# Chunk-selected attention and a squared-ReLU feed-forward on one core: every engine's order and the order of the loads fitted anew, and another price for a constant row copy

## Chip, cores and metric

The kernel runs on one core of one Trainium2 chip. The metric is the device time of one execution in microseconds (us), lower is better. The engines of a core are TensorE (PE in the profile), VectorE (DVE), ScalarE (ACT), GpSimd (POOL) and SyncE (SP). Each takes its instructions strictly in the order in which they were written for it; they wait for one another by semaphores.

## What is computed

The reference, cut to what matters (4 batches, 8 heads, 768 positions, 64 values a head; 3072 tokens, 512 wide, 2048 hidden):

```python
k_min, k_max = min and max of k over each chunk of 32 keys
ub = sum_d max(q*k_min, q*k_max)             # a bound on a chunk's scores
ub = where(chunk not after the query's, ub, -1e9)
sel = the 6 chunks with the largest ub, for each query
scores = where(sel and key <= query, (q @ k.T) / 8, -1e9)
attn_out = softmax(scores) @ v               # batch, head, position
x = attn_out as (3072, 512)
out = relu(x @ w_in)**2 @ w_out
```

## The kernel before

**Tiling.** A batch has six tiles of 128 positions. The first tile of each batch needs no selection; `first_transposes` and `first_attention` (L553 to L606) do the four of them at the start, and one feed-forward pass takes them together. The other five tiles go through 16 pairs of heads, numbered p = 0 to 15, four to a batch. `stage_a(p)` (L622 to L739) prepares a pair: keys and queries turned so that the 64 values lie on partitions (on PE in batches 0 and 1, by a transposing DMA of SP in batches 2 and 3), chunk extremes (`kr`, L697), the bounds on PE (`ub`, L660), the sixth largest of them (`m`, L668), the selection (`selb`, L727), turned as well (`sT`), and copies into the operands `kqc` and `qsc` (L281 on ACT, L283 on DVE). `stage_b(p, x)` (L766 to L821) then does, for each of the two heads, five banks of scores (`ps`, L782), the exponential on ACT (`e`, L804), the causal mask on POOL (L762) or DVE (L759), and the product with v (`av`, L793), at last the division (L612, L614) into `x`.

`ffn` (L823) runs once for the first tiles and once for each batch: `turn` (x to xT; by PE, or by SP's transposing DMAs for batches 1 to 3), `up` (`ph`, L866; ReLU `ht` on ACT, L873, or DVE, L875; square `h` on DVE, L884), `down` (`py`, L897; a copy `ob`, L281 or L283; a store by SP, L910). The feed-forward of a batch lies between and behind the attention of the next.

**The selection as a product.** The operand `kqc` has 64 rows of keys and 24 constant rows that add a large negative number for every chunk that isn't selected. These 24 x 768 constant rows are made once (L339) and copied seven times for the eight operands, the "row copies": L344 on POOL, L281 on ACT, L283 on DVE.

**What sets the order.** The kernel is written as some 1800 operations with no order of their own. `plan.op` records each with the engines it may run on and a price for each, a due time, what it needs and the buffers it uses. `Plan.order` then goes through them like a list scheduler in a model of the chip: it finds the operation that could start first, and on that engine takes, among those that could start within `wait` of it, the one with the smallest due time:

```python
first = min(found, key=lambda f: (f[0], f[1].number))
st, op, engine, cost = min(
    (f for f in found if f[2] == first[2] and f[0] <= first[0] + self.wait),
    key=lambda f: (round(f[1].due, 6), f[0], f[1].number))
```

What comes out is the order of each engine's queue, the engine for each operation that has a choice, and the buffer slots (three of `ps`, six of `e`, six of `nt`, two each of `av` and `ff`). Loads from memory are operations of POOL, whose order among themselves is the list `plan.loads`; the planner takes the next of that list when its due time beats what else POOL could do, and lets at most eight be under way. Before the 26th microsecond of its model, `Plan.order` also puts idle matmuls in front of a PE operation that must wait (`op.fill`, L539, "fillers"), to keep PE busy. They are as many as its model of the wait says; where the wait is shorter than that, they stand in the way. The due times come from a table of numbers, `P`, near the top of the kernel, and from places in a timetable of 20 units for each pair.

Loads that the prediction speaks of: the weights `w_in` in four chunks (L461), keys, queries and values of batch 0 by pairs of heads (`kn`, `qn`, `vn`, L454), first tiles of each batch (`k`, `q`, `v`, L369), whole tiles of batch 1 (L447), and `nt`, the tiles of keys and queries that SP turns by DMA for batches 2 and 3 (L434). Four first tiles (`raw`, L399) are fetched by SP itself and cast by DVE or ACT.

Of the kernel before, what the change touches and what calls it, by code (L numbers as in the profile page):

```python
# [13 lines left out]
ACT = mybir.ActivationFunctionType  # L14
# [194 lines left out]
def kernel(  # L209
# [27 lines left out]
    QC = 128 * NS  # L237
    VW = 80
    NSET = 4
    P = dict(lead=[0, 207.45, 109.14, 153.29, -29.2, 112.12, 38.49, 53.35, 112.23, 30.95,  # L240
             26.44, 98.99, 127.21, 67.89, -1.38, 124.88], f_due=[452.52,
             -1393.33, -782.42, -326.54], sp='K0 Q0 K1 Q1', rows=[-2963.23,
             -1559.78, 780.78, -565.55, 1811.92, 457.36, -1818.66, -283.78],
# [3 lines left out]
             'q3 v2 v3 k3', shift={}, p0=-2735.84, wait=0.01, xt=(1, 2, 3),  # L247
             sel=2, loads='Q3 K3 V0 V1 Q2 K2 i0 V2 k0 V3 q0 i1 k1 v2 q1 i2 '
             'v0 i3 k2 q2 o1 o0 v1 o2 k3 o3 v3 q3')

    nc.scalar.preload_act_table_set("natural_log_exp_and_others")

# [13 lines left out]
    plan = Plan({"tp": 1, "ps": 3, "av": 2, "ff": 2, "e": 6, "h2": NFI + 6, "ht": 3,  # L266
                 "ob": 3, "kq": 6, "nt": 6,
                 "vn": B - 1, "x": 2, "xT": 2,
                 "st": 2, "kr": 2, "qp": 2, "qm": 2, "ubm": 2, "m8": 2, "rc": 2}, lambda *a: keep_warm(*a), P["wait"])
    POOLS = {"tp": pst, "ps": pss, "av": psav, "ff": psf, "e": epool, "h2": hpool,  # L270
# [65 lines left out]
    def kq_rows(engine, i):  # L336
        rows = kqs[D:KC, i // 2, i % 2]
        if i == 0:
            nc.scalar.activation(  # L339
                rows.rearrange("c (a j) -> c a j", j=CH),  # L340
                ident[0:NC, 0:NC].unsqueeze(2).to_broadcast([NC, NC, CH]),
                ACT.Copy, scale=NEG)
        elif engine == "POOL":
            nc.gpsimd.affine_select(  # L344
                out=rows, in_=kqs[D:KC, 0, 0], compare_op=ALU.is_ge, fill=0.0,
                base=0, channel_multiplier=0, pattern=[[1, S]])
        else:
            copy(engine, rows, kqs[D:KC, 0, 0])

    made = {}  # L350
# [7 lines left out]
    order = []  # L358
# [93 lines left out]
    def load_pair(nm, b, hp, due):  # L452
        for h in (2 * hp, 2 * hp + 1):
            load((nm, b, hp), lambda _, h=h: nc.gpsimd.dma_start(  # L454
                out=nat[nm, b].tile[:, :, h, 0:D],
                in_=SRC[nm][b, h, 128:].rearrange("(j p) d -> p j d", p=128)),
                due, 640, [nat[nm, b]])
# [21 lines left out]

    for i, what in enumerate(P["sp"].split()):  # L480
        if what[0].isupper():
            load_by_sp(what[0].lower(), int(what[1]), -1020 + i)
        else:
            load_pair_by_sp(what[0], -1020 + i)
    made["ident"] = plan.op({"POOL": 0.75}, -997, lambda _: make_identity(nc, ident))
    made["ahead"] = plan.op({"POOL": 0.55}, -994, make_ahead)
    made["rows", 0] = plan.op({"ACT": 0.88}, P["rows"][0], lambda e: kq_rows(e, 0),
                              [made["ident"]])
    for i in range(1, 2 * NSET):
        made["rows", i] = plan.op({"POOL": 0.80, "DVE": 0.40, "ACT": 0.75}, P["rows"][i],  # L490
                                  lambda e, i=i: kq_rows(e, i), [made["rows", 0]])
    made["tri"] = plan.op({"DVE": 0.15}, -900, lambda _: nc.vector.tensor_single_scalar(
        tri, ahead, 0.0, op=ALU.is_ge), [made["ahead"]])
# [1 line left out]
    made["ubmask"] = plan.op({"DVE": 0.8}, -997, make_ubmask)  # L495
    for what in P["loads"].split():
        i = int(what[1])
# [6 lines left out]
        else:  # L504
            load_pair(what[0], 0, i, -980)
    if P["after"]:
        plan.loads[0].needs.append(made["rows", P["after"]])
# [21 lines left out]
    def keep_warm(dst, n):  # L529

        size = 1
        for dim in dst.shape[1:]:
            size *= dim
        dst = dst if len(dst.shape) == 2 else dst.rearrange(
            {3: "p a b -> p (a b)", 4: "p a b c -> p (a b c)"}[len(dst.shape)])
        if dst.dtype == F32:
            size = min(size, 512) // 128 * 128 or size
            for _ in range(n * 512 // size):
                nc.tensor.matmul(  # L539
                    dst[:, 0:size].rearrange("p (a b) -> p a b", b=min(size, 128)),  # L540
                    lhsT=warm, rhs=warm[:, 0:min(size, 128)].unsqueeze(1).to_broadcast(
                        [128, size // min(size, 128), min(size, 128)]),
                    start=True, stop=True)
        else:
            for _ in range(4 * n):
                transpose(dst[:, 0:128], warm)
# [412 lines left out]
    computed = [op for op in plan.ops if op.turns or not op.packets]  # L959
    for i, change in P["shift"].items():  # L960
        computed[i].due += change
    with tc.manual_schedule():
        plan.write()

# [29 lines left out]
```

## Time and profile before

| | |
|---|---|
| median of 3 runs | 265.79 us (264.72, 265.79, 266.02) |
| profiled execution | a span of 263.6 us from the first to the last instruction; the page gives no other time of it |
| mean granted clock of TensorE | 0.994 |
| busy: PE, DVE, ACT, POOL | 251.4, 183.0, 197.8, 106.4 us |
| instructions | 6555 |

The timed runs lie 1.1 to 2.4 us above the span of the profiled execution. Busy time counts an instruction from its start to its end; matmuls overlap their ends, so a PE that is shown as busy all the time is not at its peak. A row of a group has the line of the source, the engine, the operation, the tiles out<-in with their shapes and the count, then busy us and mean ns of one, then the idle time of the engine ahead of it and what ended most of that. Windows have, for each stretch, busy us and instructions of each engine, the granted clock of PE, and the mean use of the DMA engines.

### The profile page before, as it was taken

Reading aid. Unit: us, or ns where it says so; the run is one execution under the profiler, and the core shown is the slowest. Engines: PE = TensorE matmul, PEld = TensorE weight load, DVE = VectorE, ACT = ScalarE, POOL = GpSimd, SP = SyncE. Lnnn points to the kernel's source line nnn. Section 1 sums busy time; section 2 is a strip of 40 time slices with the busy share of each in tenths; the row PEclk is TensorE's granted clock in tenths of the full one; section 3 lists DMA queues with packets and bytes.
Section 4 is the critical chain, followed back from the end, with each engine's and each line's share of the span. In section 5 each row is a group of like instructions: output and inputs, shape, how many; then the busy total and the mean of one; then the engine's idle time right before and its main releaser. Section 6 shows DMA issues by size and latency. Waiting matters only on the chain.

```text
span 263.6 us, 6555 instructions
## 1 busy us (share of the span) xinstructions
PE 251.4 (95%) x2382; PEld 164.1 (62%) x2405; DVE 183.0 (69%) x663; ACT 197.8 (75%) x395; POOL 106.4 (40%) x185
## 2 busy tenths in 40 slices
PE   6899999999999999999999999998999999999995
PEld 1577566666687666665686645666865564765443
DVE  7569999778999999998999943644757142455000
ACT  6658897859899999999989845987866692677111
POOL 7998987799555599833311201110200010000000
PEclk9799999999999999999999999999999999999999
DMA  8999999999999999995440001154000113400122
GB/s 153 156 175 180 181 198 190 94 126 174 170 151 166 149 157 143 123 145 148 87 93 15 2 20 75 44 82 101 2 0 15 42 44 99 120 2 0 40 82 80
DMA packets 106336, 26.51 MB, mean 101 GB/s; under 512 B 99008, under 2 KB 103360, under 8 KB 106304
## 3 DMA queue, kind: packets, MB, share of 16 engines
q0 software_dynamic: 75088, 13.11, 67.9%
q1 hardware_dynamic: 31216, 12.98, 24.0%
q8 instruction: 19, 0.31, 0.5%
q14 instruction: 13, 0.11, 0.2%
HBM read 27.26 MB, written 6.29 MB: 127 GB/s over the span
## 4 chain that ended last, share of the span: by engine, by line
PE 62%; DVE 24%; ACT 8%; issue 3%; DMA 2%; SPq 0%; ACTq 0%; DVEq 0%
PE py L897 25%; PE ph L866 20%; PE ps L782 8%; PE av L793 4%; DVE h L884 4%; DVE kr L697 4%; DVE m L668 3%; DVE qsc L283 3%; ACT e L804 2%; DMA xT<-x 2%; ACT ht L873 2%; DVE x L614 2%; ACT qsc L281 2%; DVE kqc L283 1%; DVE ubm L722 1%
## 5 line engine op out<-in xcount | busy, mean ns | idle before, releaser
L866 PE MATMUL ph<-xT,w_in_sb 128*128 128x256 bf16 (+2 forms) x592 | 95.7, 304 | 1.6 <-DMA xT<-x 1.2
L804 ACT ACTIVATE e<-ps 128x512 bf16<-128x512 f32 x160 | 86.4, 608 | 7.5 <-PE ps L782 4.4
L897 PE MATMUL py<-w_out_sb,h 128*128 128x512 bf16 (+2 forms) x377 | 87.9, 370 | 1.2
L762 POOL TENSOR_SCALAR_AFFINE_SELECT e<-e 128x128 bf16<-128x128 bf16 (+1 forms) x88 | 31.0, 365 | 101.0 <-ACT e L804 89.1
L866 PEld LDWEIGHTS <-w_in_sb 128*128 128x128 bf16 x592 | 55.6, 97 | 24.9 <-DMA xT<-x 1.6
L873 ACT ACTIVATE ht<-ph 128x384 bf16<-128x384 f32 (+2 forms) x130 | 58.9, 457 | 16.2 <-PE ph L866 12.5
L884 DVE TENSOR_TENSOR h<-ht 128x256 bf16<-128x256 bf16 (+2 forms) x148 | 47.8, 333 | 16.4 <-ACT ht L873 12.9
L897 PEld LDWEIGHTS <-h 128*128 128x128 bf16 x400 | 36.2, 97 | 33.8
L782 PE MATMUL ps<-qsc,kqc 88*128 88x128 bf16 (+1 forms) x320 | 51.7, 272 | 0.3 <-DVE ubm L722 0.2
L782 PEld LDWEIGHTS <-kqc 88*128 88x128 bf16 x320 | 27.6, 97 | 14.8 <-issue 0.8
L281 ACT COPY ob<-py 128x512 f32<-128x512 f32 (+2 forms) x22 | 12.5, 570 | 29.2 <-PE py L897 29.1
L793 PEld LDWEIGHTS <-e 128*128 128x128 bf16 x640 | 29.6, 97 | 6.4 <-issue 0.3
L793 PE MATMUL av<-vn,e 128*128 128x65 bf16 x480 | 29.6, 193 | 0.0
L759 DVE TENSOR_TENSOR e<-e,tri 128x128 bf16<-128x128 bf16 (+1 forms) x40 | 9.7, 242 | 14.9 <-ACT e L804 14.2
L614 DVE TENSOR_TENSOR x<-av,rc 128x320 bf16<-128x320 f32 (+1 forms) x40 | 18.7, 472 | 0.5
L668 DVE MAX8 m<-ubm 128x8 f32<-128x24 f32 x160 | 15.5, 167 | 0.0
L697 DVE TENSOR_REDUCE kr<-kT 128x24 bf16<-128x768 bf16 x16 | 14.8, 951 | 0.2
L697 DVE TENSOR_REDUCE kr<-kt 128x24 bf16<-128x768 bf16 x16 | 14.8, 935 | 0.0
L793 PE MATMUL av<-v,e 128*128 128x65 bf16 x160 | 13.9, 193 | 0.1
L875 DVE TENSOR_SCALAR ht<-ph 128x256 bf16<-128x256 f32 (+2 forms) x18 | 8.2, 454 | 8.2 <-PE ph L866 8.2
L612 DVE RECIPROCAL rc<-av 128x5 f32<-128x5 f32 (+1 forms) x40 | 7.2, 184 | 9.4 <-PE av L793 8.5
L281 ACT COPY qsc<-sT 24x256 bf16<-24x256 bf16 (+1 forms) x29 | 12.4, 427 | 1.6 <-DMA sT<-selb 0.9
(92 smaller groups left out, 258.7 us busy)
## 6 DMA issues: line engine op xcount, KB each, us to landing
out_dram<-ob SPq DMA_DIRECT2D x23, 256.0 KB, 2.2
w_in_sb<-in_moe_w_in_dram POOLq DMA_DIRECT2D x4, 512.0 KB, 7.2
w_out_sb<-in_moe_w_out_dram POOLq DMA_DIRECT2D x4, 512.0 KB, 8.8
vn<-in_v_dram POOLq DMA_DIRECT2D x15, 128.0 KB, 6.9
nt<-in_k_dram POOLq DMA_DIRECT2D x10, 128.0 KB, 6.6
nt<-in_q_dram POOLq DMA_DIRECT2D x10, 128.0 KB, 5.3
kn<-in_k_dram POOLq DMA_DIRECT2D x8, 80.0 KB, 7.0
qn<-in_q_dram POOLq DMA_DIRECT2D x8, 80.0 KB, 5.7
```

What stands on the lines that cost most here:

```text
L281: nc.scalar.copy(dst, src)
L614: return plan.op({"DVE": 0.06 + 0.00108 * D * n}, due, lambda _: nc.vector.tensor_mul(x(), av[:, :, 0:D], rc[:, 0:n].unsqueeze(2).to_broad ...
L668: nc.vector.max(out=m8[:, i, hh], in_=ubm[:, i, hh])
L697: nc.vector.tensor_reduce(kr[:, mm].rearrange("d (t c) -> d t c", c=128 // CH) if b >= BY_DMA else kr[:, mm], part(kT).rearrange("d t (c j ...
L762: nc.gpsimd.affine_select(out=e, in_=e, compare_op=ALU.is_ge, fill=0.0, base=0, channel_multiplier=-1, pattern=[[0, n], [1, 128]])
L782: nc.tensor.matmul(ps[:, 128 * c:128 * (c + nt)], lhsT=kqs[:, s, hh, 128 * j:128 * (j + 1)], rhs=qss[:, s, hh, 128 * (t0 - 1):128 * (t0 - ...
L793: nc.tensor.matmul(av[:, t - 1], lhsT=e[:, 128 * c:128 * (c + 1)], rhs=value_tile(b, h, j), start=(i == 0 and c == 0), stop=(i == len(BANK ...
L804: nc.scalar.activation(e.tile, ps.tile, ACT.Exp, scale=scale), [sc], [ps, e])
L866: nc.tensor.matmul(ph.tile, lhsT=w_in_sb[:, ki, 128 * f:128 * (f + 1)], rhs=xT[:, c0 // 128:c1 // 128, ki], start=(ki == 0), stop=(ki == N ...
L873: nc.scalar.activation(ht.tile, ph.tile, ACT.Relu)
L884: {"DVE": 0.067 + w / 1920}, at[0] + P["h2"], lambda _: nc.vector.tensor_mul(h2[f][:, c0:c1], ht.tile, ht.tile), [op], [ht, h2[f]])))
L897: nc.tensor.matmul(py.tile, lhsT=h2[f][:, 128 * t:128 * (t + 1)], rhs=w_out_sb[:, f, c0:c1], start=(f == 0), stop=(f == NFI - 1))
```

## The change

Two things change in the table and one in a price; no computation changes, and no operation is added or taken away.

- `P["moves"]`: some 150 triples (first, last, change). Each adds a number to the due times of a run of operations that stand one after another in the program, from one operation to a few dozen or a hundred.
- `P["order"]`: another order for the 85 loads in `plan.loads`.
- the price of a row copy on DVE, 0.40 before, is 0.80; `wait` goes from 0.01 to 0.01025.

```diff
+    P.update(moves=[(404, 421, -16.62), (1023, 1024, 27.61), (1310, 1388, 35.65),
+             (1004, 1029, 6), (1072, 1086, -0.87), (1539, 1540, 6.97), (1535, 1536,
...
+             17.64)], order=[0, 2, 3, 1, 5, 4, 6, 10, 9, 8, 7, 12, 11, 13, 14, 15,
+             19, 16, 18, 20, 17, 22, 21, 23, 25, 30, 26, 24, 27, 29, 34, 31, 28, 33,
...
+             wait=0.01025)
...
     for i in range(1, 2 * NSET):
-        made["rows", i] = plan.op({"POOL": 0.80, "DVE": 0.40, "ACT": 0.75}, P["rows"][i],
+        made["rows", i] = plan.op({"POOL": 0.80, "DVE": 0.80, "ACT": 0.75}, P["rows"][i],
                                   lambda e, i=i: kq_rows(e, i), [made["rows", 0]])
...
     computed = [op for op in plan.ops if op.turns or not op.packets]
     for i, change in P["shift"].items():
         computed[i].due += change
+    for i0, i1, change in P["moves"]:
+        for op in computed[i0:i1]:
+            op.due += change
+    if P["order"]:
+        plan.loads = [plan.loads[i] for i in P["order"]]
```

Set beside each other, the two programs differ in this: of 1809 operations 96 run on another engine; of PE's 642 operations 184 keep their place in its queue and 245 more stand within three places of it; PE has 2399 matmuls instead of 2405, since 22 fillers at L539 are left of 28. In the first microseconds the first tile of batch 1 now comes ahead of that of batch 0. In the last batch, the attention of pair 14 and 15 comes earlier against the feed-forward of the batch before it.

More of the change, by code (lines that the diff above doesn't have):

```diff
@@ L239 @@
     NSET = 4
-    P = dict(lead=[0, 207.45, 109.14, 153.29, -29.2, 112.12, 38.49, 53.35, 112.23, 30.95,
+    P = dict(moves=[], order=[], lead=[0, 207.45, 109.14, 153.29, -29.2, 112.12, 38.49, 53.35, 112.23, 30.95,
              26.44, 98.99, 127.21, 67.89, -1.38, 124.88], f_due=[452.52,
```

42 rows, old and new, of the table sel are left out of this document.

## Prediction

> **What bounds the kernel now.** I read the page's head first, then the windows by stage, then what PE waited for, and last the timeline of the start, since PE is the engine that is nearly always busy.
>
> ```profile
> span 263.6 us, 6555 instructions
> PE 251.4 (95%) x2382; PEld 164.1 (62%) x2405; DVE 183.0 (69%) x663; ACT 197.8 (75%) x395; POOL 106.4 (40%) x185
> ...
> 0.00:24.00 24.00, 19.36 (x193) 13.05 (x194) 16.84 (x59) 15.98 (x26) 21.45 (x34) 0.93 1.69 163
> 24.00:70.00 46.00, 44.94 (x483) 28.90 (x487) 41.15 (x147) 37.77 (x73) 40.54 (x62) 1.00 1.68 165
> 70.00:130.00 60.00, 58.58 (x629) 40.12 (x634) 58.34 (x204) 57.84 (x115) 35.73 (x65) 1.00 1.70 143
> 130.00:260.20 130.20, 128.34 (x1085) 81.97 (x1093) 66.67 (x256) 85.92 (x182) 8.71 (x26) 1.00 0.18 48
> 260.20:263.60 3.40, 0.20 (x4) 0.02 (x1) 0.00 (x0) 0.27 (x1) 0.00 (x0) 1.00 0.22 77
> ```
>
> The columns of a window are its length, then busy us of PE, PEld, DVE, ACT and POOL with instructions, then the granted clock and the DMA traffic. PE is idle for 263.6 - 251.4 = 12.2 us: 4.64 before the 24th microsecond, 3.2 in the tail of the last store, which no order shortens, and 1.06, 1.42 and 1.86 in the three stages between, 4.3 in all. So an order can win some 9 us at the very most, and in practice a part of that. From 70 to 130 three engines are full together (58.58, 58.34 and 57.84 of 60).
>
> ```profile
> PE T L286 <- DVE k L283: 1.8, 1, 1.8
> PE ph L866 <- DMA xT<-x: 1.2, 1, 1.2
> PE xt L286 <- ACT kqc L281: 0.5, 1, 0.5
> PE ub L660 <- DVE kbd L704: 0.4, 1, 0.4
> ```
>
> These are the longest waits of PE for other engines and transfers (in all, times, longest). The first lies in the start; the one of 1.2 us is a transposing DMA that came late; then come crumbs. No stall repeats, so a refit of orders has no big prize, and the fullness of the middle gives it something to lose.
>
> **The change part by part.** PE does the same work but for six fillers, and these stand before the first feed-forward's first products for tiles 2 and 3. Behind that point the PE work is equal, so the end moves by what the start moves plus waits that come or go.
>
> *The start.* PE's rows from the 15th microsecond and ACT's up to the 24th:
>
> ```profile
> 15.74 1.70 PE L539 MATMUL ph<-warm 128*128 128x256 bf16 x14
> 17.28 1.04 PE L866 MATMUL ph<-xT,w_in_sb 128*128 128x256 bf16 x8
> 19.80 1.60 ACT L281 COPY kqc<-kT 64x768 bf16<-64x768 bf16 x2
> 20.52 0.44 PE L286 MATMUL qT<-ident,qn 128*128 128x128 bf16 x5
> 21.43 1.39 ACT L281 COPY qsc<-qT 64x640 bf16<-64x640 bf16 x2
> 21.68 1.69 PE L539 MATMUL ph<-warm 128*128 128x256 bf16 x14
> 22.84 0.59 ACT L281 COPY xT<-xt 128x512 bf16<-128x512 bf16 x1
> 23.47 1.03 PE L866 MATMUL ph<-xT,w_in_sb 128*128 128x256 bf16 x8
> ```
>
> Here are the four loads that matter: the first chunk of `w_in`, the last first tile `v`, and the queries `qn`, with one landing row for each of the three in that order.
>
> ```profile
> 9.39 0.79 POOL L461 DMA_DIRECT2D w_in_sb<-in_moe_w_in_dram  x1
> DMA to landing us min/median/max: 6.7/6.7/6.7
> 12.71 0.96 POOL L369 DMA_DIRECT2D v<-in_v_dram  x1
> DMA to landing us min/median/max: 6.8/6.8/6.8
> 13.59 1.79 POOL L454 DMA_DIRECT2D qn<-in_q_dram  x2
> DMA to landing us min/median/max: 5.8/5.9/6.1
> 1.83 0.44 POOL L422 MEMSET vn<- 128x40 bf16 x2
> ```
>
> Before, `w_in` lands at 9.39 + 6.7 = 16.1, yet the first product starts at 17.28, because 14 fillers (15.74 to 17.44, ends overlapped) stand in the way. After, POOL does one more memset of 0.22 (0.44 / 2) ahead of its loads, which was DVE's, so they start 0.2 to 0.4 later: the chunk lands near 9.7 + 6.7 = 16.4, and only 6 fillers stand ahead of the product. It starts at 16.4 to 16.6, 0.8 earlier. I don't believe that this gain is kept. The second `qn` is issued half-way through its row, at 14.49 before and about 14.7 after, and lands at 14.7 + 5.9 = 20.6 instead of 20.4. It feeds `qT` of pair 0, and behind that ACT has, in its strict order and in both kernels, the two `qsc` copies (1.39) and then an `xT` copy (0.59), for which the second products of `up` wait: 0.12 from the landing to the first transpose (20.52 against 20.4), 0.44 for them, and I allow 0.15 for the hand-overs: 20.6 + 0.71 + 1.39 + 0.59 = 23.3, against 23.43 (22.84 + 0.59) before. The 14 fillers ahead of them (1.69) end at about the same time. So the start gains 0.15: the whole 0.8 at one end; at the other a loss of 0.3, if the loads are late by their 0.4 and nothing takes it up.
>
> Row copies and casts:
>
> ```profile
> 2.97 2.29 ACT L281 COPY kqc<-kqc 24x768 bf16<-24x768 bf16 x3
> 5.96 0.91 DVE L283 CAST k<-raw 128x512 bf16<-128x512 f32 x1
> ```
>
> The doubled price sends one row copy from DVE to ACT (0.76 a copy, 2.29 / 3), two left on DVE. The cast of a key tile goes to ACT as well. Both engines have gaps there (16.84 and 15.98 busy of 24), and PE is held by loads; I cost this at nothing, covered by the load of `w_in`. If that cover is gone, a copy that stands ahead of an exponential costs its 0.76; this I leave to the slower case.
>
> *The loads behind the start.* The page's DMA row, and the last keys of batch 1, with their landing row and first use:
>
> ```profile
> DMA  8999999999999999995440001154000113400122
> 51.78 1.79 POOL L447 DMA_DIRECT2D kn<-in_k_dram  x2
> DMA to landing us min/median/max: 3.4/4.4/5.3
> 58.91 0.44 PE L286 MATMUL kT<-ident,kn 128*128 128x128 bf16 x5
> ```
>
> The second of them, issued at 52.67, lands 3.4 to 5.3 later, 58.0 at the latest, 0.9 before its use. After, it is issued about 1.1 earlier, and the first `nt` loads some 5 earlier. This removes no wait of 24 to 130 that I can name, only a part of the 2.5 us of crumbs; I take -0.3, between nothing and -1.0. By the Trainium skill, page "DMA: Bandwidth & Descriptors", section "Issuing engines are not separate DMA queues", transfers from all issuers interleave on the same 16 engines, so a load moved ahead only pushes others back. The DMA row's nines up to slice 18 agree, and by that rule alone this term would be 0.
>
> *Pairs 0 to 7, 24 to 70.* Most PE operations move a few places. One move forward matters: the fifth score bank of pair 1's second head now stands about 4 us earlier, near 43, where the exponentials
>
> ```profile
> L804 ACT ACTIVATE e<-ps 128x512 bf16<-128x512 f32 x160 | 86.4, 608 | 7.5 <-PE ps L782 4.4
> ```
>
> must free three `ps` slots at 0.608 each. If ACT is one late there, PE waits for up to one, 0.6; I take +0.2.
>
> *70 to 130.* The engines of 36 operations are swapped: 18 from ACT to DVE, 17 back, one POOL to DVE.
>
> ```profile
> L875 DVE TENSOR_SCALAR ht<-ph 128x256 bf16<-128x256 f32 (+2 forms) x18 | 8.2, 454 | 8.2 <-PE ph L866 8.2
> L283 DVE COPY qsc<-sT 24x384 bf16<-24x384 bf16 (+1 forms) x35 | 10.0, 285 | 1.3 <-PE sT L286 0.5
> ```
>
> ReLUs, seven to DVE and three back: 4 x 0.454 = +1.8 on DVE. Selection copies, three to DVE and seven back: -4 x 0.285 = -1.1. The other sixteen are net two more on DVE at up to 0.5 each, 0 to +1.0. DVE gets +0.7 to +1.7, I take +1.2; it is idle for 60 - 58.34 = 1.66. It fits, barely: 0. Bounds: -1.4, the whole idle time of PE there; and, if DVE can use none of its idle time, +1.2 to +1.7, say +1.4.
>
> *130 to the end.*
>
> ```profile
> DMA to landing us min/median/max: 2.4/2.5/5.2
> 175.44 5.17 DMA xT<-x
> ```
>
> These are the transposing DMAs of batch 2's `xT` and the late one. PE's work that covers that place is, by its queue, much the same in both kernels, so the wait of 1.2 depends on whether the transfer is late again: usually it takes 2.5. Its neighbours, not its place, decide it; I leave it in, and 0 to -1.2 as bounds. Pairs 14 and 15 now come earlier against the feed-forward of the batch before, which puts more PE work between the last `x` and its products: -0.1.
>
> Sum: -0.15 - 0.3 + 0.2 + 0 - 0.1 = -0.35, against a span of 263.6. The timed runs lie 1.1 to 2.4 above that span, the median 2.19, and nothing in the change touches what lies around it: 265.79 - 0.35 = 265.4. By the skill's rule on shared DMA engines it would be 265.7.
>
> **The rivals.**
>
> *Faster.* The late transpose is on time (-1.2), the first product's gain is kept (-0.8), the wait for `kbd` goes (-0.4): -2.4, 263.4. The wait for ACT's `kqc` may go too (-0.5), 262.9. For it: each is one wait with a row, and each can go alone. Against: the late one may come again, and ACT's chain takes back the start. Chance 0.28.
>
> *Slower: DVE becomes the bound of 70 to 130.* From the point at which its added work (0.7 to 1.7) finds none of its 1.66 idle, every DVE operation behind is late, squares `h` first, and PE waits for them at `down`: +1.4, with a late start of +0.3, 267.5. For it: DVE's waits there are for PE, which is as full, so idle time may lie in the wrong places. Against: ACT gets lighter by as much. Chance 0.18.
>
> *Slower: a second slow-clock window at the start.*
>
> ```profile
> 5.20:8.60 3.40, 1.23 (x17) 0.91 (x19) 2.84 (x6) 1.28 (x4) 3.40 (x5) 1.00 1.93 185
> 8.60:12.00 3.40, 3.24 (x30) 2.04 (x27) 1.51 (x4) 2.57 (x5) 3.40 (x5) 0.51 2.33 150
> 12.00:15.50 3.50, 2.96 (x47) 1.99 (x47) 2.83 (x10) 1.67 (x3) 3.50 (x5) 0.99 1.44 180
> ```
>
> A stretch in which PE was busy for 1.23 of 3.4 is followed by one at a clock of 0.51; busy for 3.24 there, it has 0.99 in the next. If the new order of the first tiles leaves PE less busy from 8.6 to 12.0, the 2.96 us of work from 12.0 to 15.5 takes twice as long; the 0.54 idle there and 0.7 of the 0.9 before the first product (16.4 after, so 15.5 to 16.4) take some of it: +1.7, 267.5. The Trainium skill, page "TensorE: Matmul & The Clock Gate", section "What's actually happening", has one idle window of about 3.4 us halve the rate and one busy window restore it; these rows agree. Chance 0.06.
>
> *The loads and orders do nothing* that reaches PE: no change, 265.8. This is inside the forecast's own case, chance 0.48 with it.
>
> **How the numbers follow.** A measurement of this kernel can tell about 0.5%, 1.33 us, from no change: faster is below 264.46, slower above 267.12. The likeliest case is 265.4, its own range 264.4 to 266.9. The faster case reaches 262.9, the slower ones 267.5, so the range is 262.9 to 267.6. Of the likeliest case's 0.48, 0.03 falls on the faster side and 0.01 on the slower one by the bounds of its terms: faster 0.28 + 0.03 = 0.31, slower 0.18 + 0.06 + 0.01 = 0.25, same 0.44. Some 1 in 10 each stays out below and above the range.
>
> **What would show it.** In the changed kernel's profile: the first `up` at 16.4 to 16.6 and the second at about 23.3; if the second is at 22.7, ACT's chain was no bound. A clock near 0.5 in one 3.4 us window only. DVE near 59.5 busy of 60 from 70 to 130, with PE still at 58 or more; a PE wait for `h` there would show the second rival. PE's wait for `xT` near 1.2, or gone. New waits of PE for exponentials at 42 to 46. It is wrong if a stage behind the 24th microsecond has over 1 us more or less of PE idle time than before.

## The result, and the profile after

The changed kernel takes 264.82 us in the median of 18 runs (263.01 to 267.96), the kernel before 265.99 beside it; the ratio is 0.9948, with a 95% interval of 0.9927 to 0.9970. That is 1.4 us faster (0.8 to 1.9), at the bound of what a measurement can tell. Here and below, a run over 1.5% above the fastest of its kernel is left out of the ratio: one of the changed kernel's, two of `early_moves`, four of `no_fill`. The forecast was 265.4, 0.35 faster: the direction is right, the size a quarter of what came.

The page of the changed kernel, and its windows by stage (columns as before; the last one is the tail). Its lines lie 47 further down: L539 is now L586, L866 L913, L897 L944.

```profile
span 262.3 us, 6546 instructions
PE 253.6 (97%) x2399; PEld 164.7 (63%) x2399; DVE 183.1 (70%) x663; ACT 195.7 (75%) x393; POOL 106.5 (41%) x187
...
0.00:24.00 24.00, 19.94 (x187) 13.41 (x188) 16.55 (x58) 16.20 (x26) 20.90 (x34) 1.00 1.65 161
24.00:70.00 46.00, 45.60 (x489) 29.07 (x487) 42.06 (x150) 36.52 (x71) 40.84 (x63) 1.00 1.90 174
70.00:130.00 60.00, 59.67 (x635) 40.42 (x634) 57.99 (x205) 58.12 (x116) 35.72 (x66) 1.00 1.66 138
258.90:262.30 3.40, 0.00 (x0) 0.00 (x0) 0.00 (x0) 0.00 (x0) 0.00 (x0) 1.00 0.23 81
```

PE shows 2.2 us more busy time than before, although six idle matmuls are gone. That is no work; it is the records. Before has 2382 matmuls for 2405 weight loads, after 2399 for 2399, and the group of `down` tells where the 23 missing ones were (before, then after):

```profile
L897 PE MATMUL py<-w_out_sb,h 128*128 128x512 bf16 (+2 forms) x377 | 87.9, 370 | 1.2
```

```profile
L944 PE MATMUL py<-w_out_sb,h 128*128 128x512 bf16 (+2 forms) x400 | 91.5, 370 | 0.0
```

So idle times of PE can't be compared between the two pages. What can be: the weight loads, which are complete in both, each taken with the columns that its matmul streams (four products of 512 columns span 1.02 us here, the last of them 0.37, so one starts each 0.217 us).

```profile
43.13 1.02 PE L913 MATMUL ph<-xT,w_in_sb 128*128 128x512 bf16 x4
```

Laid out so, each kernel has a time at which a given amount of PE work is still to come. The difference to before's profile, in us, for the changed kernel and for four of the experiments below:

```
before at   after  early_moves  start_only  no_loads  store_later
 28.6 us    +0.1      +0.6        +0.7        +0.1       +0.1
 60.9       -0.2      +0.3        +0.4        -0.1       -0.1
 93.2        0.0      +0.5        +0.6        +0.3       +0.1
100.6       -1.1      -0.6        -0.4        +0.3       +0.1
126.4       -0.6      -0.2        -0.3        +1.1       +0.1
158.0       -0.7      -0.4        +0.3        +3.9       +0.1
176.8       -0.6      -0.4        +0.3        +3.8       +0.1
184.4       -2.0      -1.0         0.0        +2.8       -0.7
260.1       -2.0      -0.9        +0.5        +2.9       -0.7
```

In this pair of profiles the changed kernel gains nothing at the start, 1.1 between 93 and 101 us, gives 0.5 of it back by 126, and gains 1.4 between 177 and 184, where before waited for the late transpose. From there on the two run in step. PE ends 2.0 earlier, the span only 1.3: the last store, of 64 KB, takes 2.3 us to land instead of 1.6. One pair is not enough to call these places the cause: the last section shows profiles of equal queues that differ by 0.6 and 0.7 us.

PE's longest waits after:

```profile
PE wt L586 <- DVE warm L398: 1.1, 1, 1.1
PE T L333 <- ACT t L328: 1.0, 2, 0.7
PE T L333 <- DVE q L330: 0.6, 1, 0.6
PE ps L630 <- DVE t L330: 0.5, 1, 0.5
PE qT L333 <- DMA qn<-in_q_dram: 0.3, 1, 0.3
PE ph L913 <- ACT xT L328: 0.3, 1, 0.3
```

The waits for `kbd` (0.4) and for the DMA `xT` (1.2) are off the list; what is left lies in the start. The first of these waits stands in the profile of before as well (1.1, at L539), where the prediction's list leaves it out.

### The profile page after: what moved, and what is told of

Same layout as the page of the kernel before. It is cut to its first block, busy times and chain, and to the rows that moved or that the text cites. A ratio compares the mean times of both kernels' runs of the same rounds, so it can differ in the third digit from the quotient of the medians.

```text
span 262.3 us, 6546 instructions
## 1 busy us (share of the span) xinstructions
PE 253.6 (97%) x2399; PEld 164.7 (63%) x2399; DVE 183.1 (70%) x663; ACT 195.7 (75%) x393; POOL 106.5 (41%) x187
## 4 chain that ended last, share of the span: by engine, by line
PE 82%; DVE 5%; POOL 5%; ACT 3%; DMA 2%; issue 1%; ACTq 0%; POOLq 0%
PE py L944 30%; PE ph L913 29%; PE ps L829 13%; PE av L840 7%; DMA qn<-in_q_dram 2%; ACT qsc L328 1%; POOL v L416 1%; PE qT L333 1%; DVE kr L744 1%; PE kT L333 1%; PE ub L709 1%; POOL k L416 1%; PE ub L707 1%; POOL kn L501 1%; DVE m L715 1%
## 5 line engine op out<-in xcount | busy, mean ns | idle before, releaser
L913 PE MATMUL ph<-xT,w_in_sb 128*128 128x256 bf16 (+2 forms) x592 | 96.5, 304 | 0.4 <-ACT xT L328 0.3
L944 PE MATMUL py<-w_out_sb,h 128*128 128x512 bf16 (+2 forms) x400 | 91.5, 370 | 0.0
L913 PEld LDWEIGHTS <-w_in_sb 128*128 128x128 bf16 x592 | 55.5, 97 | 22.9 <-issue 0.7
L920 ACT ACTIVATE ht<-ph 128x256 bf16<-128x256 f32 (+2 forms) x129 | 58.4, 455 | 14.3 <-PE ph L913 10.7
L944 PEld LDWEIGHTS <-h 128*128 128x128 bf16 x400 | 36.1, 97 | 33.7
L829 PE MATMUL ps<-qsc,kqc 88*128 88x128 bf16 (+1 forms) x320 | 53.0, 272 | 0.2
L328 ACT COPY ob<-py 128x512 f32<-128x512 f32 (+2 forms) x19 | 10.7, 565 | 30.1 <-PE py L944 30.0
L840 PE MATMUL av<-vn,e 128*128 128x65 bf16 x480 | 30.7, 193 | 0.1
L922 DVE TENSOR_SCALAR ht<-ph 128x256 bf16<-128x256 f32 (+2 forms) x19 | 9.2, 483 | 10.4 <-PE ph L913 10.4
L328 ACT COPY qsc<-sT 24x256 bf16<-24x256 bf16 (+1 forms) x33 | 13.9, 420 | 0.7
L494 POOL DMA_DIRECT2D vn<-in_v_dram x15 | 13.4, 904 | 0.0
```

The lines of the kernel that those rows point to most:

```text
L328: nc.scalar.copy(dst, src)
L829: nc.tensor.matmul(ps[:, 128 * c:128 * (c + nt)], lhsT=kqs[:, s, hh, 128 * j:128 * (j + 1)], rhs=qss[:, s, hh, 128 * (t0 - 1):128 * (t0 - ...
L840: nc.tensor.matmul(av[:, t - 1], lhsT=e[:, 128 * c:128 * (c + 1)], rhs=value_tile(b, h, j), start=(i == 0 and c == 0), stop=(i == len(BANK ...
L913: nc.tensor.matmul(ph.tile, lhsT=w_in_sb[:, ki, 128 * f:128 * (f + 1)], rhs=xT[:, c0 // 128:c1 // 128, ki], start=(ki == 0), stop=(ki == N ...
L920: nc.scalar.activation(ht.tile, ph.tile, ACT.Relu)
L944: nc.tensor.matmul(py.tile, lhsT=h2[f][:, 128 * t:128 * (t + 1)], rhs=w_out_sb[:, f, c0:c1], start=(f == 0), stop=(f == NFI - 1))
```

## Experiments

Theory 1: the gain is made of two waits that the profile of before shows, that for the late transpose at 180 us and the one at 94 to 101. Theory 2: it is made in the orders of the first 130 us, together with the loads, and the two waits are partly one run's.

**More cover for the transposes, in the kernel before** (`xt_cover`):

```diff
-                    [xT] + xs, late=-1.0))
+                    [xT] + xs, late=1.5 if rows[0] == 2 * S + 128 else -1.0))
```

> The kernel before, planned with batch 2's transposes of x counted as 2.5 us slower: 1.7 us more PE work stands between that x and its first products, nothing else moves. Theory 1 (the wait of 1.2 us for the late transpose is in most runs of before, and it is most of what the refit saves): the wait at that place is gone, 1.0 to 1.2 us faster than before, about 264.8. Theory 2 (the late transpose was one run's, and the refit saves in the stages before 130 us): within 0.4 us of before.

Ratio to before 0.9969 (0.9943 to 0.9995): 0.8 faster, between 0.1 and 1.5. PE no longer waits at that place. So the wait is in more than one run, and worth something. It isn't so that nothing else moves: from 175 to 212 us the queues are planned anew, and 17 operations run on another engine.

**The moves by operation number** (`late_moves`, `early_moves`): the list split at 1100.

```diff
+    late_moves:  moves=[x for x in MOVES if x[0] >= 1100], order=[], row price 0.40
+    early_moves: moves=[x for x in MOVES if x[0] < 1100], order=ORDER, row price 0.80
```

> Only those moves that concern operations from pair 9 on (numbers from 1100), loads and row price as before: before up to about 105 us, near the refitted order after that; PE's cover of batch 2's transposes is 6.2 us, that of the last batch 10.2. Theory 1: the same transfers come with the same cover as in the refitted kernel, so most of its gain of 1.4, 0.8 to 1.4 us faster. Theory 2: nothing, within 0.4 us of before.

> The other part: all loads, the row price, and the moves of operations numbered below 1100; the rest as before. The cover of batch 2's transposes falls to 5.45 us, 0.9 less than before. Theory 1: the start and the middle give 0.1 to 0.4, and the shorter cover takes 0.3 to 0.9 if that transfer is late again: 0 to 0.8 slower than before. Theory 2: 0.8 to 1.4 us faster.

Late: 0.9999 (0.9969 to 1.0030). Early: 0.9955 (0.9931 to 0.9979), nearly the whole gain, although the cover of the transposes is shorter and PE waits 0.5 for them:

```profile
PE ph L913 <- DMA xT<-x: 0.5, 1, 0.5
```

By the ratios alone that is theory 2. But 6 of the 12 runs of `late_moves` have a mean clock below 0.983, and 9 of the 35 of before beside them; such runs take some 1.5 us more (see "The second slow window" below). The other six of `late_moves` have a median of 264.84, the other 26 of before 265.50. At the same clock the late moves are thus 0.7 faster, as much as `xt_cover`. And in the profile of `early_moves`, 0.6 of its 0.9 comes between 177 and 184 us, at the transposes. So these two runs don't decide between the theories.

**No idle matmuls** (`no_fill`): `if st < self.FILL and fresh` becomes `if False and fresh`.

> The refitted kernel without any of its 22 idle matmuls at L586. By the prediction's step the start is bound by loads and ACT's chain of copies: the second products of the first feed-forward stay at 23.3 to 23.6 us, the first ones come at 16.4 to 16.6, the whole time changes by less than 0.4 us. Rival (the idle matmuls hold the clock): a second window near half clock, the second products 0.7 to 1.7 us later, as much slower in all. Rival (the idle matmuls stand in the way): the second products near 22.7, 0.5 to 0.8 faster.

1.0000 to before (0.9965 to 1.0035): the refit's gain is gone. The median of all twelve runs is 266.68, against 265.69 beside it. Eight of the twelve have a mean clock below 0.983 and a median of 267.08, the other four 265.14: the clock is the cause. Here are windows of its start (the profiled run is its fourth longest, 267.37, with a span of 265.6):

```profile
15.50:18.90 3.40, 1.05 (x8) 0.80 (x9) 0.16 (x1) 1.49 (x4) 1.66 (x3) 0.96 2.04 150
18.90:22.30 3.40, 2.18 (x17) 1.65 (x17) 1.61 (x7) 0.62 (x2) 1.94 (x3) 0.50 1.69 187
22.30:25.70 3.40, 2.77 (x28) 2.35 (x27) 2.48 (x9) 2.93 (x5) 3.40 (x5) 0.54 1.74 125
```

and from its timeline PE's products of the first feed-forward, with the wait ahead of each in brackets:

```profile
17.67 1.05 PE L913 MATMUL ph<-xT,w_in_sb 128*128 128x256 bf16 x8 [2.39 <-DMA w_in_sb<-in_moe_w_in_dram]
20.53 1.90 PE L913 MATMUL ph<-xT,w_in_sb 128*128 128x256 bf16 x8
26.77 0.49 PE L913 MATMUL ph<-xT,w_in_sb 128*128 128x256 bf16 x3 [1.27 <-ACT xT L328]
```

PE waits 2.39 for `w_in`, is busy 1.05 of 3.4 us, and then runs at half rate for two windows; eight products take 1.90 instead of 1.05, and the second products start at 26.77. The expectation that this changes under 0.4 fell; the rival "they hold the clock" stands.

**The start and the loads alone** (`start_only`): only the moves numbered below 404, all loads, the row price.

> All loads, the row price, and only the moves of operations numbered below 404: every queue is that of the refitted kernel up to 56 us and near that of before from there on. The cover of batch 2's transposes is 5.1 us, 1.2 less than before. Theory 1 (half of the refit's gain is the wait at those transposes, half the waits of 94 to 101 us): no better than before at the same clock, 0 to 0.8 slower where that transfer is late. Theory 2 (the gain is the start, which no longer falls into three slow-clock windows, and the loads): the whole gain of the early part, 0.8 to 1.4 us faster, and no run with a mean clock below 0.983.

1.0021 (0.9995 to 1.0046). No gain, and 1.7 us behind `early_moves` by the two ratios. The two differ only in the due times of operations numbered from 404 to 1100, of some 57 to 130 us; but the planner orders what lies behind anew as well, and the queues differ up to 213 us. In the table above they stand level at 126 us (-0.2 and -0.3), and the gap opens behind that. Theory 2's form "it is the start and the loads" fell too. No run fell below a mean clock of 0.983.

**One reduction later in DVE's queue** (`kr_later`): in the kernel before, `moves=[(1153, 1154, 8)]` alone.

> The kernel before with one due time changed: the reduction of 0.9 us for pair 11 (kr) that stands ahead of kbd of pair 8 in DVE's queue at 99 us comes behind it. Theory 1: PE's bounds of pair 8 wait no more, the 1.0 us that PE falls behind between 94 and 101 us shrinks to 0.4 or less, 0.5 to 0.9 us faster than before. Theory 2: DVE is full there, so the same microsecond turns up elsewhere before 130 us: within 0.3 us of before.

1.0070 (1.0038 to 1.0102), 1.9 us slower. The edit changes one due time, but not one place alone: the queues of all engines differ from before's between 95 and 165 us, and 32 operations run on another engine. So it is no clean trial of that stall, and my reading of it is neither shown nor refuted. PE's wait for `kbd` left the list, and others came (its waits from 90 to 180 us):

```profile
PE ph L913 <- DVE ht L922: 1.0, 1, 1.0
PE ph L913 <- ACT ht L920: 0.5, 1, 0.5
PE ps L829 <- ACT e L851: 0.3, 1, 0.3
```

Little of the 1.9 is the clock at the start, which is below 0.983 in 4 of its 12 runs: the others have a median of 266.94, those of before 265.17.

**More cover in the changed kernel, and the row price alone** (`after_cover`, with the line of `xt_cover`; `price_only`, with no moves and no order).

> The refitted kernel, planned with batch 2's transposes of x counted as 2.5 us slower: their cover on PE is 7.7 us instead of 6.2. Theory 1 (that transfer is late in a part of the runs of both kernels, by up to 1.2 us more than the cover): 0.3 to 0.6 faster than the refitted kernel, 1.7 to 2.0 faster than before. Theory 2 (the refit's transposes are on time as a rule): within 0.2 of the refitted kernel, 1.2 to 1.6 faster than before.

> The kernel before with the price of 0.80 for a row copy on DVE, and the new wait, and nothing else of the change; the order behind 24 us is nearly the one of before. The prediction costs the row copies at nothing: within 0.3 us of before. Rival: a copy more on ACT ahead of the first exponentials, 0.76 slower. For the theory on the transposes: their cover is 6.3 us as before, so this profile shows once more whether the wait of about 1.2 us comes there (theory 1: 0.3 to 1.2).

`after_cover`: 0.9944 (0.9918 to 0.9969), the same as the refit, which fits transposes that are on time there as a rule. It is the lowest ratio of all, but no better than the change within its interval. `price_only`: 0.9986 (0.9955 to 1.0017), no change that can be told. Its queues are those of before from 26 us on, and its wait for the DMA `xT` is 0.9:

```profile
PE ph L913 <- DMA xT<-x: 0.9, 1, 0.9
```

**The store behind the transposes** (`store_later`): in the kernel before, one place of SP's queue.

```diff
+                if getattr(op, "behind", None) and op.behind not in done:
+                    continue
...
+    plan.ops[1046].behind = plan.ops[1349]
```

> The kernel before with one thing moved: in SP's queue the store (L957) that is issued 0.8 us ahead of batch 2's five transposes of x comes behind them. Theory 1 (the store's 256 KB delay the second transpose, and its lateness of 0.9 to 1.2 us in PE's waits is in most runs): that transpose lands in about 2.5 to 3 us, PE's wait at it is gone, 0.8 to 1.2 us faster than before. Rival (the transpose is late by itself or by something else): PE still waits about 0.9 to 1.2 there, within 0.3 us of before.

In its profile PE waits 0.34 instead of 1.2 (a row of its timeline, then the landing row of all its `xT` transposes):

```profile
179.95 0.61 PE L915 MATMUL ph<-xT,w_in_sb 128*128 128x256 bf16 x4 [0.34 <-DMA xT<-x]
```

```profile
DMA to landing us min/median/max: 2.4/2.5/4.4
```

but the ratio is 1.0006 (0.9980 to 1.0032). The slowest transpose still takes 4.4 us, so the store is not all of its lateness, and 0.8 us in one profile became nothing over 12 runs.

**The old row price in the changed kernel** (`after_oldprice`): 0.80 back to 0.40; three row copies and a memset change engine, nothing else behind 4 us.

> The refitted kernel with the price of a row copy on DVE back at 0.40: three row copies and one memset stand on the engines that they had before, PE's queue and everything behind 4 us are the refitted kernel's. Theory A (the row price keeps the start out of runs with three slow-clock windows): some 3 of 12 runs have a mean clock below 0.983 and take 1.2 us more; the median is 0 to 0.4 slower than the refitted kernel. Theory B (the order of first tiles and loads does that): no run below 0.983, within 0.2 of the refitted kernel, and a little faster where POOL's loads start 0.2 earlier.

0.9975 (0.9947 to 1.0003), and no run of 12 below a clock of 0.983: theory B, as far as 12 runs tell.

**The moves without the loads** (`no_loads`: moves numbered from 450, no order; `middle_only`: of these only up to 1100; both with the row price).

> The change without its order of the loads and without the moves of operations numbered below 450: the start and the loads of before (with the new row price), the moves of pairs 2 to 15. PE's order up to 70 us is that of before. Theory 1 (the gain is in the middle and the late orders): 1.0 to 1.8 us faster than before, as the start of before is 0.5 better than the refitted one. Theory 2 (the orders pay only with the loads moved forward): at most 0.5 us faster than before.

> The same without the moves numbered from 1100: only the orders from about 60 us to 130 us are fitted anew, and the cover of batch 2's transposes falls to 5.45 us. Theory 1 (the middle alone gives 0.6 to 1.0, the shorter cover takes 0.3 to 0.9 of it): 0.8 us faster to 0.2 slower. Theory 2 (what the early moves won they won by the loads): 0.3 to 0.9 slower than before, by the cover.

1.0112 (1.0086 to 1.0139) and 1.0093 (1.0064 to 1.0122): 3.0 and 2.5 us slower than before. Neither expectation reaches that far. Two windows of `no_loads`, and four of PE's longest waits in it:

```profile
100.00:130.00 30.00, 29.19 (x328) 18.36 (x332) 27.00 (x109) 28.34 (x55) 15.79 (x33) 1.00 1.47 127
130.00:160.00 30.00, 28.28 (x276) 19.66 (x276) 28.48 (x121) 27.13 (x58) 5.51 (x16) 1.00 0.17 37
```

```profile
PE ph L913 <- ACT ht L920: 1.1, 2, 0.7
PE ph L913 <- DVE ht L922: 0.6, 3, 0.3
PE ps L829 <- ACT e L851: 0.5, 1, 0.5
PE sT L333 <- DVE selb L774: 0.5, 2, 0.3
```

and the same windows of the changed kernel:

```profile
100.00:130.00 30.00, 29.91 (x315) 18.46 (x314) 28.41 (x109) 29.48 (x57) 14.00 (x34) 1.00 1.35 132
130.00:160.00 30.00, 29.97 (x260) 19.79 (x259) 23.54 (x106) 22.58 (x50) 3.23 (x9) 1.00 0.13 38
```

Without the new order of loads DVE and ACT do less work up to 130 us and 4.9 and 4.6 us more behind it; PE then waits for both. The loads of `nt` are what differs most: the keys of the last pairs are read from 102.84 us on in `no_loads` and from 95.69 in the changed kernel.

```profile
102.84 0.90 POOL L481 DMA_DIRECT2D nt<-in_k_dram  x1
105.06 3.53 POOL L481 DMA_DIRECT2D nt<-in_k_dram  x4
```

```profile
95.69 0.89 POOL L481 DMA_DIRECT2D nt<-in_k_dram  x1
97.68 0.92 POOL L481 DMA_DIRECT2D nt<-in_k_dram  x1
101.30 0.88 POOL L481 DMA_DIRECT2D nt<-in_k_dram  x1
105.38 0.88 POOL L481 DMA_DIRECT2D nt<-in_k_dram  x1
```

That the moves from 450 on cost time without the rest of the change is shown. `no_loads` lacks the order of the loads and also 34 moves, those numbered below 450 (two of them, at 404 and 422, are in `start_only` neither), and no run parts the two. So it is argued that the loads make the difference, and that it is these of `nt` among them.

**At the same clock.** Some runs of before and of kernels with its start have a mean clock below 0.983, and how many differs from one set of rounds to the next. These are the medians of the runs in the ratio without them, beside those of before in the same rounds, in us:

```
                runs   median   before   difference
xt_cover         11    264.75   265.50     -0.8
late_moves        6    264.84   265.50     -0.7
early_moves      10    264.54   265.50     -1.0
after_cover      12    264.10   265.17     -1.1
after_oldprice   12    264.62   265.15     -0.5
price_only       12    265.08   265.17     -0.1
start_only       12    266.13   265.17     +1.0
```

With so few runs each difference is good to 0.3 to 0.7 us.

## Why the prediction was right, and where it was not

**Direction and bound.** The time lies in the range, and the kernel got faster; that the sum came near is in part luck, as the terms show. It held that no stall repeats and that an order can win little. 1.4 us is little. It also held that 4.3 us of idle PE lay in the middle stages; with 23 matmul records missing from that page, this was not a measure of what could be won. The count stood in the quoted line (x2382 against x2405). Its last sign of being wrong, over 1 us more or less idle time of PE in a stage behind 24 us, did come: by the weight loads PE is 1.4 quicker behind 130 us.

**The start, -0.15: near in size by luck, wrong in its steps.** The second products start at 23.56 against 23.47, so nothing was gained, and ACT's chain does hold them, as the step said (`PE ph <- ACT xT`, 0.3). But `w_in` takes 7.4 us to land, not 6.7, and the first products come at 17.05 instead of 16.4 to 16.6. And the profile after had no slow-clock window, that of before one. With one such window `early_moves`, which has the same start, stands 0.6 later than before at 28.6 us, beyond the bound of +0.3.

**Row copies at nothing: right.** `price_only` is within its interval of 1.

**Loads -0.3, pairs 0 to 7 +0.2, 70 to 130 at 0: these are the terms that failed.** They were priced one by one and added. The runs show that they don't add: loads with the start +0.5 us (`start_only`; +1.0 at the same clock), the moves behind them without these +3.0 (`no_loads`), all together -1.4. The order of DVE and ACT in the dense stretch seems fitted for loads that come earlier (the last four keys of `nt` by 2 to 9 us). The prediction looked only for waits that the moved loads would take away, and found none. By the rule that it took from the Trainium skill ("DMA: Bandwidth & Descriptors", section "Issuing engines are not separate DMA queues") they were worth nothing; with the new start alone they gained nothing. From 28.6 to 60.9 us the changed kernel gains 0.3, and the new wait for exponentials that gave the +0.2 is not on PE's list.

**DVE's idle 1.66 from 70 to 130: it fits, as forecast.** DVE is busy 57.99 there, less than before, not the 59.5 that I worked out: the +1.2 us of swapped operations doesn't show in that window. The rival in which DVE becomes the bound did not come in the changed kernel; in `no_loads` something of its kind did, for ACT as for DVE.

**The late transpose, left in: wrong for the profile, open for the runs.** It is gone in the profile after, with a cover on PE of 6.2 us against 6.3, so the order there is not the reason. Cover for it alone gave 0.8 (0.1 to 1.5), moving the store, which took most of the wait out of the profile, nothing (between 0.5 faster and 0.9 slower). The rival "faster" named this wait, the one for `kbd` and the first products' 0.8; the third did not come. The -0.1 for pairs 14 and 15 doesn't show: from 184 us on the two kernels run in step.

**The second slow window: a real mechanism, on the other kernel.** Of 93 runs of before, 21 had a mean clock below 0.983, and their median is 266.74 against 265.28 for the others: 1.5 us, near the 1.7 worked out. Of 66 runs of kernels with the new start and its idle matmuls none had. Since 21 of 93 by 1.5 is 0.33, that is about 0.3 us of the mean gain in the long run. In the measurement of the result it is likely more: the clocks of its 18 runs of before aren't on record, but 8 of them took over 266.3 us, and of the 20 such runs among the 93, 18 had the low clock; 8 of 18 by 1.5 is 0.7, an estimate. `late_moves` shows such a start, slow from 8 to 16 us:

```profile
5.20:8.60 3.40, 1.53 (x15) 1.01 (x17) 2.66 (x5) 1.27 (x4) 3.40 (x5) 0.81 1.97 179
8.60:12.00 3.40, 3.35 (x30) 2.10 (x31) 1.70 (x4) 2.65 (x5) 3.40 (x5) 0.50 2.20 143
12.00:15.50 3.50, 2.96 (x36) 2.37 (x35) 2.31 (x9) 1.14 (x3) 3.50 (x5) 0.50 1.38 166
```

By the condition of the prediction (PE less busy from 8.6 to 12.0) this should not have happened, with 3.35 of 3.4 busy. The Trainium skill, "TensorE: Matmul & The Clock Gate", section "What's actually happening", says that the windows run free; that would fit, but no trace here shows where a window begins. What keeps a start out of it is not single: the new start had none with the old row price either (0 of 12, `after_oldprice`), and the old order of loads had none with the new row price (0 of 24 in `price_only`, `no_loads` and `middle_only`).

What stays open: of the 1.4 us, 0.3 to 0.7 are the clock. The rest, 0.7 to 1.1, is about what cover for the transposes (`xt_cover`) or the late moves gain by themselves at the same clock, 0.7 to 0.8; but `early_moves`, which leaves 0.5 of that wait in place, gains 1.0 as well. So the runs don't settle how much of it is the wait at the transposes and how much is made by loads and orders together.

## What to carry to other kernels

A schedule that was fitted as a whole is judged as a whole: parts of this one, run alone, gave +3.0, +0.5 and 0.0 us, and together -1.4. One changed due time orders much behind it anew, so such an edit tests more than the place that it names. Loads that take away no wait by themselves may be what allows another order of the engines behind them; here that is argued, not shown apart. Before idle time is read as headroom, compare matmuls with weight loads on the page; and a wait of a microsecond in one profile is to be tried by a run that removes it, with many rounds, before it is called the cause. Where the clock at the start differs from run to run, two ratios are set against each other only with that taken out.

## What the runs showed of the hardware

The same queues don't run the same. From 26 to 102 us the queues of before, `xt_cover`, `store_later`, `price_only` and `late_moves` are equal, and POOL issues five loads of `vn` in a row near 93 us. One DVE instruction there took 0.87 or 0.88 us in the first three and 0.33 or 0.34 in the last two (before and `price_only`):

```profile
93.69 0.87 DVE L713 TENSOR_SCALAR qp<-qt 128x640 bf16<-128x640 bf16 x1
```

```profile
94.18 0.34 DVE L760 TENSOR_SCALAR qp<-qt 128x640 bf16<-128x640 bf16 x1
```

The reduction `kr` that follows a few instructions later starts at

```profile
98.93 0.91 DVE L697 TENSOR_REDUCE kr<-kt 128x24 bf16<-128x768 bf16 x1
```

```profile
98.85 0.91 DVE L744 TENSOR_REDUCE kr<-kt 128x24 bf16<-128x768 bf16 x1
```

so DVE took 5.24 us for this stretch before and 4.67 in `price_only`. Where it was short, PE's loss between 94 and 101 us was 0.6 less. So more than half of the 1.1 that the changed kernel gains there over before comes in `price_only` and `late_moves` without any new order there. `xt_cover`, whose queues are before's up to 175 us, falls back by a further 0.7 between 129 and 135, and nothing here says why. The Trainium skill, "SBUF — State Buffer", section "SBUF: two separate sides", has DVE and GpSimd share a port pair that one of them holds for a whole instruction; the rows fit that, and no run here tested it. Also unexpected was how much a start without idle matmuls loses: 8 of 12 runs of `no_fill` had a mean clock below 0.983.
